# Attention block, one core: normalised rows taken off ScalarE, and the whole plan of instructions replaced

## Chip, core and metric

The kernel runs on one core of one Trainium2 chip. The metric is the device time of one execution in microseconds, from the core's own records. A core has TensorE (PE) for matmuls with a queue of its own for loading weights (PEld), VectorE (DVE), ScalarE (ACT), GpSimd (POOL) and SyncE (SP), which here only issues DMAs. Each engine takes its instructions in order and waits on semaphores where the program says so. Matmul results land in PSUM, which has 8 banks of 512 float32 per partition; everything else lies in SBUF, 128 partitions wide.

## What is computed

One pre-norm transformer layer over 2048 rows of 640 values, with a linear attention of 32 heads of width 20 and a gated bilinear feed-forward of width 1536. Cut to what matters:

```python
def _layernorm(x, axis=-1, eps=1e-5):
    m = jnp.mean(x, axis=axis, keepdims=True)
    v = jnp.var(x, axis=axis, keepdims=True)
    return (x - m) / jnp.sqrt(v + eps)

def _A_ref(x, wqkv, w_phi, wo):          # S = 2048, D = 640, H = 32, Dh = 20
    qkv = (x @ wqkv).reshape(B, S, 3, H, Dh).transpose(2, 0, 3, 1, 4)
    q, k, v = qkv[0], qkv[1], qkv[2]
    pq = jnp.einsum("bhsd,hdf->bhsf", q, w_phi)
    pk = jnp.einsum("bhsd,hdf->bhsf", k, w_phi)
    phi_q = jnp.concatenate([softmax(pq), softmax(-pq)], axis=-1)
    phi_k = jnp.concatenate([softmax(pk), softmax(-pk)], axis=-1)
    kv = jnp.einsum("bhsf,bhsd->bhfd", phi_k, v)
    z  = jnp.einsum("bhsf->bhf", phi_k)
    num = jnp.einsum("bhqf,bhfd->bhqd", phi_q, kv)
    den = jnp.einsum("bhqf,bhf->bhq", phi_q, z)[..., None] + 1e-6
    return (num / den).transpose(0, 2, 1, 3).reshape(B, S, D) @ wo

def _B_ref(x, w_gate, w_up, w_down):      # F = 1536
    return ((x @ w_gate) * (x @ w_up)) @ w_down

h  = x + _A_ref(_layernorm(x), A_wqkv, A_w_phi, A_wo)
h2 = h + _B_ref(_layernorm(h), B_w_gate, B_w_up, B_w_down)
```

All inputs and the output are bfloat16.

## The kernel before

**Tiles and steps.** The 2048 rows are 16 tiles of 128. The program first builds a graph of about a thousand named steps, most of them one instruction, and each with an engine, the buffers that it reads and writes, and sometimes a second engine that can do it as well (`alts`). The table `PLAN` then gives each step by name its place in one common order, which of its engines it runs on (the second field: empty or 0 for the first, 1 for the alternative) and which slots of its pools it uses (the third field: PSUM banks, or slots of ring buffers). `arrange` sorts the steps by place and hands each engine its own list; `emit` works out the semaphore waits from the buffers. So the plan alone sets the order on each engine and on the SP queue, and with the order it sets who waits for whom: an instruction that waits holds up all that stands behind it on its engine.

**Names.** The number behind a name is the row tile. For layer norm: `L1s` (VectorE, two statistics instructions, lines 406 and 407), `L1a` (VectorE, aggregate to mean and variance, line 409), `L1l` and `L1e` (ScalarE, logarithm and exponential that give 1/sqrt, lines 414 and 417, for one, two or four tiles at a time), `L1n` (the shift: minus mean times that factor, one value per row, line 421, GpSimd or VectorE) and `xn` (the normalised row tile, lines 424 to 434). `xn` on VectorE subtracts the mean and multiplies by the factor (line 431), and needs no shift; on ScalarE it is an activation with scale and bias (line 429), and the bias is the shift. Tiles 2 and 9 run on ScalarE in this plan. All tiles from 2 on have a shift, whether or not they use it, and `xn` waits for it as one of its inputs.

`xt` transposes the normalised tile: tiles 0 and 1 on TensorE (line 440, with the evacuation `xte`), the others by a DMA from the SP queue (line 449). That queue also issues the loads of x (`x8` and so on), of the feed-forward weights (`wg`, `wu`, `wd`, line 263) and of `wo`, the transposed loads of the query weights `wqt`, and later the transposes `qT`, `oT` and `hT`.

**The key and value stage.** `WT` and `F1_` fold the feature map w_phi into the key weights (transposes at line 370, folds at line 389, evacuations `WTe` and `Fe1_` at line 229; `Ph` builds the block form of w_phi and `w5` loads it); `F0_` does it for the query weights. `V` and `K` of a tile are ten matmuls each (line 460), for tiles 0 and 1 in five pieces. `Ve` evacuates V (line 229, ScalarE or VectorE). For K come two exponentials on ScalarE (`Kx_0` and `Kx_1`, line 472), a sum on VectorE (`Ks`, line 476), logarithm and exponential on ScalarE (`Kr` and `Ke`, lines 479 and 481, the reciprocal) and a product on GpSimd (`Kn`, line 496). `KV` adds the tile to the 32 heads' state in two PSUM banks that all 16 tiles share (line 504). The buffers of `xn` are four slots, those of the exponentials five.

**The rest.** `Q` has steps of the same kind (`Qx` at lines 529 and 531, `Qs` at 534, `Qr`, `Qb`, `Qe`, `Qn` at 537 to 548, `qT` at 553). Behind `KVe` (line 511), which needs the last `KV`, come `N` (line 566), the division `dd`, `rd`, `o`, the transpose `oT`, `O` (line 603), the sum `h` (line 609), the centred copy `hc` and its transpose `hT`. The feed-forward has five bands of rows; `U` are the gate and up products (line 646), `g` and `u` their evacuations, `D` the down product (line 665), `y` the last sum and `w` the store.

**Where the plan puts the steps that matter below.** TensorE goes through `... V3 K5 V5 K2 V2 V4 F0_0 ...`, later `... K6 K9 Q0 Q1 KV4 K8 KV5 Q5 K11 ...`, and at the end of the stage `KV11 KV12 KV13 KV14 KV15 Q6 N0`. The SP queue goes `... xt6 xt7 x10 x14 wg2 wg0 xt9 wd1 xt8 wg1 xt11 wd0 xt13 xt10 ...`. GpSimd goes `... Kn1 L1n7 L1n6 rqz Kn3 L1n8 L1n9 Kn0 mk0 mk1 Kn2 ...` and ends the stage with `... Kn12 Qb4 Kn14`.

## Time and profile before

| | us |
|---|---|
| three timed runs | 271.76, 271.76, 272.92 |
| median of the three | 271.76 |
| the profiled execution | 272.37 |
| its span, first to last instruction | 270.6 |
| granted TensorE clock over the span | 1.000 |

Times are in microseconds unless marked ns. In a row of the timeline stand the start, the length, the engine, the line of the kernel, the operation, what it writes and reads, the shape, and how many instructions were merged; in brackets how long the engine had been idle before it, and on whom it had waited. Matmuls are pipelined, so their row is longer than the time between two of them. A row of the groups has busy time and mean ns of one instruction, then the idle time just before the group's instructions and who ended most of it. `SPq` is the time in which the SP queue issues a DMA, not the transfer itself. A row of the stretches gives the stretch, its length, and the busy time of PE, PEld, DVE, ACT and POOL with their instructions, then the granted clock, the DMA share and GB/s.

### The profile page before, as it was taken

What the parts mean: (1) busy time and instruction counts of PE and PEld (TensorE: products, weight loads), DVE (VectorE), ACT (ScalarE), POOL (GpSimd) and SP (SyncE); (2) the same over time, 40 slices, a digit from 0 to 9 for tenths busy, and PEclk for the clock granted to TensorE, in tenths of its full rate; (3) what the DMA queues carried; (4) which work ended last, traced back from release to release, by engine and by line L of the source; (5) the groups of instructions that cost most, each with busy time, mean ns of one, the idle gap of its engine ahead of it and who ended that gap; (6) DMA issues with size and microseconds to landing.
All of it is one profiled execution on the core that took longest, in us unless ns stands there. A gap on an engine that the chain in (4) does not pass through costs nothing.

```text
span 270.6 us, 5179 instructions
## 1 busy us (share of the span) xinstructions
PE 263.6 (97%) x2090; PEld 177.4 (66%) x2103; DVE 157.3 (58%) x291; ACT 123.9 (46%) x316; POOL 71.8 (27%) x92
## 2 busy tenths in 40 slices
PE   6999989999999999999999999999999999999996
PEld 4777857777777788765556667765554476544774
DVE  4999799967678998678564252432342411433432
ACT  3899979988876383663531051223122300023000
POOL 6155689999942422205000000000000000000000
DMA  7999996999947997882940000240200001100011
GB/s 210 307 122 172 250 226 132 298 207 253 174 87 145 166 139 133 134 145 55 188 84 2 0 0 25 61 112 1 73 12 2 0 0 51 48 1 0 27 48 61
DMA packets 71752, 28.09 MB, mean 104 GB/s; under 512 B 59056, under 2 KB 71728, under 8 KB 71728
## 3 DMA queue, kind: packets, MB, share of 16 engines
q1 hardware_dynamic: 71440, 27.43, 49.7%
q8 instruction: 16, 0.26, 0.4%
q10 hardware_dynamic: 288, 0.33, 0.3%
q14 instruction: 8, 0.07, 0.1%
HBM read 11.00 MB, written 2.62 MB: 50 GB/s over the span
## 4 chain that ended last, share of the span: by engine, by line
PE 91%; DMA 4%; DVE 2%; ACT 1%; issue 0%; DVEq 0%
PE ps L646 38%; PE ps L460 23%; PE ps L665 19%; PE ps L603 7%; DMA xnT<-xn 3%; PE ps L566 2%; PE ps L504 2%; DMA x_all<-in_A_x_dram 1%; DVE x_all L609 1%; DVE S L534 1%; PE ps L389 1%; DVE st L406 0%; ACT Wp L229 0%; DVE st L407 0%; ACT scratch L229 0%
## 5 line engine op out<-in xcount | busy, mean ns | idle before, releaser
L646 PE MATMUL ps<-xnT,Wgu 128*128 128x512 bf16 (+1 forms) x587 | 106.0, 335 | 0.7
L646 PEld LDWEIGHTS ps<-xnT,Wgu 128*128 128x128 bf16 x600 | 58.2, 98 | 43.5
L651 ACT ACTIVATE gt<-ps 128x512 bf16<-128x512 f32 (+1 forms) x60 | 29.7, 509 | 100.9 <-PE ps L646 62.9
L460 PE MATMUL ps<-Wp,xnT 128*128 128x320 bf16 (+1 forms) x480 | 68.9, 299 | 1.1 <-DMA xnT<-xn 1.1
L460 PEld LDWEIGHTS ps<-Wp,xnT 128*128 128x128 bf16 x480 | 45.3, 97 | 18.7 <-DMA xnT<-xn 1.7
L654 DVE TENSOR_TENSOR ev<-ps,gt 128x512 bf16<-128x512 f32 (+1 forms) x60 | 33.6, 580 | 36.5 <-PE ps L646 27.8
L665 PE MATMUL ps<-Wd,ev 128*128 128x320 bf16 (+2 forms) x396 | 53.9, 295 | 0.0
L665 PEld LDWEIGHTS ps<-Wd,ev 128*128 128x128 bf16 x396 | 38.1, 98 | 15.3 <-DVE ev L654 0.2
L677 DVE SCALAR_TENSOR_TENSOR Wp<-ps,rs,x_all 128x640 bf16<-128x640 f32 (+3 forms) x18 | 14.6, 810 | 49.3 <-PE ps L665 49.1
L496 POOL TENSOR_TENSOR ek<-ek,SR 128x1280 bf16<-128x1280 bf16 x16 | 37.6, 2356 | 5.5 <-ACT SR L481 5.5
L534 DVE TENSOR_REDUCE S<-ph 128x66 f32<-128x1320 bf16 x16 | 23.9, 1517 | 4.6 <-ACT ph L531 4.5
L476 DVE TENSOR_REDUCE SR<-ek 128x64 f32<-128x1280 bf16 x16 | 23.3, 1470 | 3.0 <-ACT ek L472 3.0
L529 ACT ACTIVATE ph<-ps 128x600 bf16<-128x600 f32 x32 | 21.4, 682 | 7.8 <-PE ps L460 7.1
L603 PE MATMUL ps<-Wo,Wp 128*128 128x320 bf16 x160 | 23.7, 299 | 0.1
L548 POOL TENSOR_TENSOR ph<-ph,RQ 128x660 bf16<-128x660 bf16 x16 | 20.7, 1307 | 8.7 <-ACT RQ L544 8.4
L472 ACT ACTIVATE ek<-ps 128x640 bf16<-128x640 f32 x32 | 21.3, 720 | 3.3 <-PE ps L460 2.6
L624 POOL TENSOR_SCALAR ln<-mv 128x1 f32<-128x1 f32 x12 | 2.3, 190 | 75.7 <-ACT ek L620 75.1
L603 PEld LDWEIGHTS ps<-Wo,Wp 128*128 128x128 bf16 x160 | 15.4, 98 | 6.1 <-issue 0.2
L609 DVE SCALAR_TENSOR_TENSOR x_all<-ps,x_all 128x640 bf16<-128x640 f32 x16 | 13.1, 821 | 6.1 <-PE ps L603 6.1
L593 DVE TENSOR_TENSOR o<-ps,sm 128x660 bf16<-128x660 f32 x16 | 13.4, 840 | 1.0 <-ACT sm L586 0.6
L620 ACT ACTIVATE ek<-x_all,mv 128x640 bf16<-128x640 bf16 x16 | 13.1, 820 | 0.0
L229 ACT ACTIVATE ev<-ps 128x640 bf16<-128x640 f32 x16 | 11.2, 705 | 1.3 <-PE ps L460 1.3
(68 smaller groups left out, 158.1 us busy)
## 6 DMA issues: line engine op xcount, KB each, us to landing
out_dram<-Wp SPq DMA_DIRECT2D x15, 160.0 KB, 1.8
x_all<-in_A_x_dram SPq DMA_DIRECT2D x6, 320.0 KB, 4.5
Wgu<-in_B_w_gate_dram SPq DMA_DIRECT2D x4, 480.0 KB, 6.7
Wd<-in_B_w_down_dram SPq DMA_DIRECT2D x4, 480.0 KB, 5.0
Wgu<-in_B_w_up_dram SPq DMA_DIRECT2D x4, 480.0 KB, 5.7
Wp<-in_A_wqkv_dram SPq DMA_DIRECT2D x5, 160.0 KB, 4.7
ev<-in_A_wqkv_dram SPq DMA_DIRECT2D x4, 160.0 KB, 3.7
x_all<-in_A_x_dram SPq DMA_DIRECT2D x3, 160.0 KB, 3.3
```

Of the source, the lines that this page charges most:

```text
L460: ins = e.matmul(pb(b, hb)[:, 0:n1 - n0], lhsT=T["xnT"][:, NC - 1 - c, P * t:P * (t + 1)], rhs=T["Wp"][:, POS[kind], c, n0:n1], start=(c = ...
L472: G.op("act", "%sx%d_%d" % (nm, t, s), lambda e, s=s, b=b, ek=ek: e.activation(out=T["ek"][:, ek.slots[0], 0:2 * D].rearrange("p (b h s f) ...
L476: G.op("dve", "%ss%d" % (nm, t), lambda e, ek=ek, sr=sr: e.tensor_reduce(out=T["SR"][:, sr.slots[0], 0, :], in_=T["ek"][:, ek.slots[0], 0: ...
L496: G.op("pool", "Kn%d" % t, lambda e, eng, ek=ek, sr=sr: e.tensor_tensor(out=T["ek"][:, ek.slots[0], 0:2 * D].rearrange("p (h f) -> p h f", ...
L529: e.activation(out=v[:, 0:10].rearrange("p (b g) j f -> p b g j f", b=2), in_=pp(b, 0, 300).rearrange("p b (g j f) -> p b g j f", j=3, f=D ...
L534: G.op("dve", "Qs%d" % t, lambda e, t=t, ph=ph: e.tensor_reduce(out=T["S"][:, t, 0:66].rearrange("p (g k) -> p g k", k=6), in_=pv(ph).rear ...
L548: return e.tensor_tensor(out=v, in0=v, in1=T["RQ"][:, rq.slots[0], 1, 0:33].rearrange("p (g j) -> p g j", j=3).unsqueeze(3).to_broadcast([ ...
L603: ins = e.matmul(pb(b, hb)[:, 0:320], lhsT=T["oT"][:, oT.slots[0], c, :], rhs=T["Wo"][:, c, 320 * hb:320 * (hb + 1)], start=(c == 0), stop ...
L646: ins = e.matmul(pb(b)[:, 0:n], lhsT=T["Wgu"][:, gu, c, P * ft:P * (ft + 1)], rhs=T["xnT"][:, NC - 1 - c, o0:o0 + n], start=(c == 0), stop ...
L651: G.op("act", "g%d_%d" % (bi, ft), lambda e, pg=pg, gt=gt, n=n: e.activation(out=T["gt"][:, gt.slots[0], 0:n], in_=pb(pg)[:, 0:n], func=AF ...
L654: o_ = G.op("dve", "u%d_%d" % (bi, ft), lambda e, pu=pu, gt=gt, hh=hh, ft=ft, n=n: e.tensor_tensor(out=T["hh"][:, hh.slots[0], ft, 0:n], i ...
L665: ins = e.matmul(pb(b, hb)[:, 0:w], lhsT=T["hh"][:, hh.slots[0], ft, P * tt:P * (tt + 1)], rhs=T["Wd"][:, ft, c0 + w * hb:c0 + w * (hb + 1 ...
```

## The change

Three things. `xn` loses its ScalarE form; its alternative engine is now GpSimd, with the same instruction as on VectorE. The shift steps `L1n` (14 of them), their buffer and `xn`'s wait for them are gone. And `PLAN` is replaced as a whole: 1014 steps instead of 1028.

In the new plan `xn4` and `xn6` run on GpSimd and all other rows on VectorE. ScalarE's queue issues the loads `x1 x3 wk1 w5` (it had `x1 wk3`). `Ve8`, `Ve10`, `Ve11`, `Ve14` and `Ve15` move from ScalarE to VectorE; `WTe0` moves to ScalarE, `xte1` and `Ph1` to VectorE; some of `Fe0_`, `hc` and the small `L2v` change places too. TensorE has the same 295 steps in another order. It starts with `V0_0 V0_1 F1_2 V0_2 K1_0 ...` behind the first four folds, then `K3 V3 K5 V5 V2 K2 V4 F0_0 F0_2 V6 ...`, `... K6 KV2 F0_1 K9 KV3 Q1 Q0 ... K8 KV5 Q5 K11 V9 Q3 Q9 ...`. ScalarE goes `... Ve3 L1l6 Kr0 L1e6 Kx5_0 Kr1 Kx5_1 L1l8 Ke0 Ve5 L1e8 Ve2 Ke1 Ve1 Kx2_0 ...`, VectorE `... WTe4 xte1 xte0 WTe2 xn3 L1s4 L1s5 L1a4 L1a5 xn5 L1s2 L1a2 L1s7 L1s6 xn2 L1a7 L1s9 L1a6 Ks0 L1s8 Ks1 xn7 L1a8 L1a9 Ks3 ...`, GpSimd `... phz ekz xn4 xn6 mk0 Kn0 Kn1 Kn3 mk1 Kn2 mk2 Kn4 Kn5 Kn7 Kn6 Qb1 Kn9 ...` up to `Kn13 Kn12 Kn14`, and the SP queue `... xt6 xt7 x14 x10 wo0 xt9 wu1 xt8 wu2 wd1 wg0 xt11 wg3 xt10 ...`. From `KV11` to `N0` TensorE's order is the old one, and so are its last seven steps.

The plan's lines with the first steps and with the steps named in the prediction, and then the code:

```diff
--- before.py
+++ after.py
-x0:0 x1:1:1 ekz:2 zero:3 id0:4 warm0:5 wk3:6:1 x3:7:1 warm1:8 id1:9 warm2:10 w5:11:1 warm3:12 va1:13 warm4:14 warm5:15 wk0:16:1 warm6:17 warm7:18 eps:19
...
-Ks1:123::0 K0_3:124 L1e2:125 Ve0:126::0 V1_2:127 L1n2:128 xt5:129 V1_3:130 Sz:131 L1n4:132 xn2:133:1:0 V1_4:134 K3:135::4 L1s6:136 Kr1:137 wqt0:138 Ke1:139
...
-L1e6:156 wqt2:157 Ve3:158::2 L1n7:159 L1n6:160 rqz:161 Kx0_0:162::2 V5:163::0 xn7:164::2 Kx0_1:165 xt4:166 xn6:167::3 Kx5_0:168::3 L1a8:169 K2:170::6 L1a9:171
-Ks0:172::2 Kx5_1:173 wqt3:174 Kr3:175 Ke3:176 V2:177::2 Ve5:178::3 Kn3:179 Ks5:180::3 xt6:181 Kx2_0:182::4 Kx2_1:183 V4:184::4 L1s12:185 xt7:186 Ve2:187::4
-L1l8:188 Ks2:189::0 L1e8:190 Kr0:191 F0_0:192::0 L1n8:193 x10:194 Ke0:195 F0_2:196::6 L1n9:197 Ve4:198::5 Kn0:199 V6:200::2 x14:201 L1s13:202 Fe0_0:203
-wg2:204 xn9:205:1:0 wg0:206 F0_4:207::4 K4:208::0 Kr5:209 Fe0_4:210:1 xt9:211 Ve6:212::6 mk0:213 Kr2:214 mk1:215 Ke2:216 Fe0_2:217 KV0:218::4,5 Kn2:219
...
-L1s15:251 Kr4:252 Ve7:253::7 K9:254::6 L1n10:255:1 L1a13:256 Ke4:257 xn11:258::3 Kx6_0:259::4 L1a15:260 L1a12:261 xt11:262 Kx6_1:263 Ks7:264::2 Kn4:265
...
+zero:0 va1:1 x0:2 x1:3:1 warm0:4 x3:5 wk4:6:1 warm1:7 warm2:8 eps:9 gl0:10 wk3:11 wk1:12:1 warm3:13 id0:14 warm4:15 warm5:16 w5:17 wk0:18:1 gla:19 warm6:20
...
+L1a7:139 L1s9:140 xt2:141 L1a6:142 V3:143::0 Ks0:144::0 Kx3_0:145::4 Kx3_1:146 xt4:147 K5:148::6 L1s8:149 Ve3:150::1 L1l6:151 wqt0:152 Ks1:153::1 Kr0:154
...
+mk0:171 Kn0:172 K2:173::6 L1e8:174 Ve2:175::3 L1s13:176 xt6:177 Ke1:178 Ve1:179::4 Ks5:180::3 V4:181::4 Kx2_0:182::3 xt7:183 Kx2_1:184 Kn1:185 L1s12:186
...
+K4:203::6 Ke2:204 xn9:205::3 Ve6:206::6 Fe0_3:207:1 xt9:208 Ke5:209 Fe0_0:210:1 KV0:211::0,1 KV1:212 mk1:213 Kx4_0:214::1 wu1:215 K7:216::4 Kn2:217 xt8:218
...
+wg0:235 L1s11:236 Ke4:237 KV2:238 Kn4:239 F0_1:240::6 Kx6_0:241::3 K9:242::2 L1s14:243 Kx6_1:244 L1a12:245 L1a11:246 Fe0_1:247 L1a10:248 Ks7:249::0 KV3:250
...
+Ks6:266::1 L1l12:267 Q1_4:268 xt11:269 Ke7:270 Q0_2:271 Qx1_0:272::4 KV4:273 Q0_3:274 Kn7:275 Qx1_1:276 Q0_4:277 Ks9:278::2 K8:279::2 Kr6:280 Qx0_0:281::1
...
@@ -244,7 +244,6 @@
     st_b = [Buf("st%d" % t) for t in range(NT)]
     mv_b = [Buf("mv%d" % t) for t in range(NT)]
     rs_b = [Buf("rs%d" % t) for t in range(NT)]
-    nb_b = [Buf("nb%d" % t) for t in range(NT)]
     wkn_b = [Buf("wkn%d" % i) for i in range(NC)]
     wkt_b = [Buf("wkt%d" % i) for i in range(NC)]
     wqt_b = [Buf("wqt%d" % g) for g in range(NC)]
@@ -416,22 +415,14 @@
              [lb], 10 * a - 26)
         G.op("act", "L1e%d" % a, lambda e, a=a, z=z: e.activation(out=T["rs"][:, a:z], in_=T["ln"][:, a:z], func=AF.Exp,
                                                                  scale=-0.5), 0.1, LA, [lb], [rs_b[t] for t in tl], 10 * a - 26)
-        for t in tl:
-            if t > 1:
-                G.op("pool", "L1n%d" % t, lambda e, eng, t=t: e.tensor_scalar(
-                    out=T["nb"][:, t:t + 1], in0=T["mv"][:, t, 0:1], scalar1=T["rs"][:, t:t + 1], scalar2=-1.0, op0=ALU.mult,
-                    op1=ALU.mult), 0.2, LP, [rs_b[t], mv_b[t]], [nb_b[t]], 10 * t - 25, alts=[("dve", 0.07, LD)])
     KVB = [Buf("kvps%d" % k, "psum") for k in range(2)]
     for t in range(NT):
         xb = Buf("xn%d" % t, "xn")
         def xn(e, eng="dve", t=t, xb=xb):
-            if eng == "act":
-                return e.activation(out=rev(xb), in_=T["x"][:, t, :].rearrange("p (c n) -> p c n", c=NC), func=AF.Identity,
-                                    scale=T["rs"][:, t:t + 1], bias=T["nb"][:, t:t + 1])
             return e.tensor_scalar(out=rev(xb), in0=T["x"][:, t, :].rearrange("p (c n) -> p c n", c=NC),
                                    scalar1=T["mv"][:, t, 0:1], scalar2=T["rs"][:, t:t + 1], op0=ALU.subtract, op1=ALU.mult)
-        G.op("dve", "xn%d" % t, xn, 0.5, LD, [x_b[t], mv_b[t], rs_b[t], nb_b[t]], [xb], 10 * t - 22,
-             alts=[] if t < 2 else [("act", act_c(640, True), LA)])
+        G.op("dve", "xn%d" % t, xn, 0.5, LD, [x_b[t], mv_b[t], rs_b[t]], [xb], 10 * t - 22,
+             alts=[] if t < 2 else [("pool", 0.95, LP)])
         if t in TPE:
             b = Buf("pxt%d" % t, "psum")
             def xt(e, t=t, b=b, xb=xb):
@@ -827,7 +818,6 @@
         T["mv"] = sb([P, NT, 2], FP32, "mv")
         T["mv2"] = sb([P, NT, 2], FP32, "mv2")
         T["ln"] = sb([P, NT], FP32, "ln")
-        T["nb"] = sb([P, NT], FP32, "nb")
         T["rs"] = sb([P, NT], FP32, "rs")
         T["rs2"] = sb([P, NT], FP32, "rs2")
         T["SR"] = sb([P, NSLOTS["SR"], 2, 2 * H], FP32, "SR")
```

More of the change, by code (lines that the diff above doesn't have):

```diff
@@ L122 @@
[L122 to L123 removed]
+zero:0 va1:1 x0:2 x1:3:1 warm0:4 x3:5 wk4:6:1 warm1:7 warm2:8 eps:9 gl0:10 wk3:11 wk1:12:1 warm3:13 id0:14 warm4:15 warm5:16 w5:17 wk0:18:1 gla:19 warm6:20
+id1:21 warm7:22 wk2:23:1 warm8:24::4 glb:25 warm9:26 rqz:27 smz:28 wv1:29 Sz:30 warm10:31 warm11:32 wv0:33:1 warm12:34 L1s0:35 warm13:36 x4:37 warm14:38
@@ new lines @@
+mk0:171 Kn0:172 K2:173::6 L1e8:174 Ve2:175::3 L1s13:176 xt6:177 Ke1:178 Ve1:179::4 Ks5:180::3 V4:181::4 Kx2_0:182::3 xt7:183 Kx2_1:184 Kn1:185 L1s12:186
+F0_0:187::2 Kr5:188 Kr3:189 Ve4:190::5 F0_2:191::6 x14:192 Ks2:193::0 V6:194::0 Ke3:195 x10:196 Fe0_2:197 wo0:198 Kn3:199 xn8:200::1 F0_3:201::4 Kr2:202
+K4:203::6 Ke2:204 xn9:205::3 Ve6:206::6 Fe0_3:207:1 xt9:208 Ke5:209 Fe0_0:210:1 KV0:211::0,1 KV1:212 mk1:213 Kx4_0:214::1 wu1:215 K7:216::4 Kn2:217 xt8:218
+Kx4_1:219 Ks4:220::1 V7:221::6 Kx7_0:222::0 wu2:223 Kx7_1:224 wd1:225 mk2:226 L1s10:227 F0_4:228::2 Ve7:229::4 K6:230::4 L1s15:231 Fe0_4:232 Kr4:233 L1a15:234
@@ new lines @@
+Qx10_0:421::0 Qx10_1:422 V14:423::2 Kr14:424 Kn12:425 Qx13_0:426::1 Qs10:427 Qe4:428 V12:429::6 Ve14:430:1:3 Qr10:431::1 qT5:432::4 Ke14:433 Qx13_1:434
+Kn14:435 V15:436::2 Ve12:437::2 Qs13:438 wg1:439 KV11:440 Ve15:441:1:4 KV12:442 Qr13:443::0 KV13:444 Qb13:445 Qb10:446 Qe13:447 KV14:448 Qn4:449 KV15:450
+Q6:451::2 KVe0:452 Qn13:453 KVe1:454 Qx6_0:455::2 N0:456::4 N2:457::0 qT4:458::2 dd0:459::0 Qx6_1:460 Q7:461::6 rd0:462 dd2:463::1 o0:464::0 rl2:465 rd2:466
+o2:467::1 N1:468::2 Qx7_0:469::5 Q11:470::4 dd1:471::1 oT0:472::0 Qx7_1:473 rd1:474 o1:475::2 Q8:476::0 Qx11_0:477::3 oT2:478::1 Qs7:479 Qx11_1:480 N3:481::2
```

120 lines of the change are left out of this document (57 added, 63 removed).

## The prediction

> **What bounds the kernel now.** I read the page first, then the timeline of TensorE, then the timelines of the engines and of the DMA queue that feed it in the first 80 us.
>
> ```profile
> span 270.6 us, 5179 instructions
> PE 263.6 (97%) x2090; PEld 177.4 (66%) x2103; DVE 157.3 (58%) x291; ACT 123.9 (46%) x316; POOL 71.8 (27%) x92
> PE 91%; DMA 4%; DVE 2%; ACT 1%; issue 0%; DVEq 0%
> ...
> 7.12 0.45 PE L440 MATMUL ps<-ident,xn 128*128 128x128 bf16 x5 [0.72 <-DVE xn L431]
> ...
> 10.27 0.48 PE L389 MATMUL ps<-Phi,scratch 128*128 128x140 bf16 x6 [0.19 <-ACT Wp L229]
> 10.58 15.23 PE L460 MATMUL ps<-Wp,xnT 128*128 128x320 bf16 x110
> ...
> 24.28 1.20 PEld L460 LDWEIGHTS ps<-Wp,xnT 128*128 128x128 bf16 x10 [0.28 <-DMA xnT<-xn]
> ...
> 36.63 4.26 PE L460 MATMUL ps<-Wp,xnT 128*128 128x320 bf16 x30 [1.07 <-DMA xnT<-xn]
> 36.62 3.38 PEld L460 LDWEIGHTS ps<-Wp,xnT 128*128 128x128 bf16 x26 [1.40 <-DMA xnT<-xn]
> ...
> 250.04 18.20 PE L665 MATMUL ps<-Wd,ev 128*128 128x320 bf16 x144
> ```
>
> TensorE is 97% busy and is 91% of the chain that ended last. From 10.58 us to 268.24 (250.04 + 18.20) it streams with only two waits worth a name: 0.28 us at 24.28 (step V4 waits for the transposed rows of tile 4) and 1.40 us on the weight loads at 36.62 (step K9 waits for those of tile 9; about 1.36 net, as two steps stand about 0.04 apart anyway). The new order has the same 295 TensorE steps and the same matmuls. So the change can win only what those waits and the first 10.6 us hold, about 2 us, and can lose by any new wait.
>
> **The change, part by part, in its arithmetic.**
>
> ```profile
> L431 DVE TENSOR_SCALAR xn<-x_all,mv,rs 128x640 bf16<-128x640 bf16 x14 | 8.1, 587 | 0.3
> L421 POOL TENSOR_SCALAR nb<-mv,rs 128x1 f32<-128x1 f32 x9 | 2.3, 265 | 10.5 <-ACT rs L417 10.5
> L429 ACT ACTIVATE xn<-x_all,nb,rs 128x640 bf16<-128x640 bf16 x2 | 1.8, 912 | 0.0
> L421 DVE TENSOR_SCALAR nb<-mv,rs 128x1 f32<-128x1 f32 x5 | 1.0, 203 | 0.0
> L548 POOL TENSOR_TENSOR ph<-ph,RQ 128x660 bf16<-128x660 bf16 x16 | 20.7, 1307 | 8.7 <-ACT RQ L544 8.4
> L229 ACT ACTIVATE ev<-ps 128x640 bf16<-128x640 f32 x16 | 11.2, 705 | 1.3 <-PE ps L460 1.3
> L476 DVE TENSOR_REDUCE SR<-ek 128x64 f32<-128x1280 bf16 x16 | 23.3, 1470 | 3.0 <-ACT ek L472 3.0
> ```
>
> Removed: 14 shifts (9 on GpSimd, 2.3 us; 5 on VectorE, 1.0 us) and 2 rows on ScalarE (1.8 us). VectorE keeps 14 rows of 0.59 us: it takes over tiles 2 and 9 from ScalarE and gives 4 and 6 to GpSimd. A GpSimd row isn't in the trace. It costs more than the 0.27 us of a one-element GpSimd instruction and not more than the 1.31 us of a two-input one of 660 elements; I take 1.0, as it has one big input. By itself none of this is on TensorE's path: the rows of tiles 4 and 6 are needed at 24 and 26 us. The plan also moves five evacuations of V (tiles 8, 10, 11, 14, 15) from ScalarE (0.70 us each) to VectorE. They are covered: VectorE stands idle 2.43, 1.83 and 2.12 us between 58 and 71 us (rows below), against 5 x 0.82 = 4.1. Without that cover VectorE would be late by up to 4.1 us for the key sums. What decides is the new order.
>
> ```profile
> 60.08 1.53 DVE L534 TENSOR_REDUCE S<-ph 128x66 f32<-128x1320 bf16 x1 [2.43 <-ACT ph L531]
> ...
> 64.97 1.49 DVE L476 TENSOR_REDUCE SR<-ek 128x64 f32<-128x1280 bf16 x1 [1.83 <-ACT ek L472]
> ...
> 71.39 2.96 DVE L534 TENSOR_REDUCE S<-ph 128x66 f32<-128x1320 bf16 x2 [2.12 <-ACT ph L531]
> ...
> 28.17 0.82 DVE L229 CAST Wp<-ps 128x640 bf16<-128x640 f32 x1 [0.65 <-PE ps L389]
> ```
>
> *Start (to 10.6 us).* ScalarE's queue now issues four loads instead of two, so key weights are queued earlier; but the first rows still wait for the first x (2.90 us of VectorE's idle time, all before 3.96), and then for two statistics and ScalarE's two small steps. The last fold now stands behind two V pieces (2 x 0.27 us) that are work anyway. One evacuation more in line on VectorE, one fewer wait on ScalarE: I take +0.1. Bounds: -0.7 (all of the 0.72 wait at 7.12 gone) and +0.7 (one more ScalarE evacuation of 0.70 in line).
>
> *K2 and V4 (22 to 25 us).* ScalarE now has the logarithm of tile 1's sums (Kr1) ahead of the second exponential of K5, and the statistics of tiles 8 and 9 (L1l8) ahead of the evacuations of V5 and V2. Both wait for VectorE, and everything behind them in ScalarE's queue waits too: K2 and V4 take over those PSUM banks.
>
> ```profile
> 9.90 0.48 DVE L406 BATCH_NORM_STATS2 st<-x_all 128x6 f32<-128x320 bf16 x1
> 10.30 0.48 DVE L407 BATCH_NORM_STATS2 st<-x_all 128x6 f32<-128x320 bf16 x1
> ...
> 22.44 0.29 ACT L479 ACTIVATE SR<-SR 128x64 f32<-128x64 f32 x1
> 22.76 0.26 ACT L481 ACTIVATE SR<-SR 128x64 f32<-128x64 f32 x1
> 22.92 0.69 ACT L229 ACTIVATE ev<-ps 128x640 bf16<-128x640 f32 x1
> 23.50 1.29 ACT L472 ACTIVATE ek<-ps 128x640 bf16<-128x640 f32 x2
> ```
>
> VectorE begins the statistics of tile 4 at 9.90 now; a part of Phi more stands ahead of them (Ph1) and the start is +0.1 late, so I take 10.5. Up to the end of Ks1 stand seven pairs of statistics (0.79 each, from 9.90 to 10.69), five aggregates (about 0.17), two rows and two sums: 5.5 + 0.85 + 1.2 + 2.9 = 10.5, and about 0.9 of waits for ScalarE: Ks1 ends near 21.9. Then Kr1 0.25 and the exponential 0.6 to 0.7: K2's banks are free at 22.9, where TensorE comes at 22.7. Ks1 plus a row and two aggregates gives 22.8 for L1l8; by the starts above (0.3, 0.16, 0.58, 0.2, 0.6 to 0.7) the evacuation of V2 ends at 24.95. V4 starts there instead of at 24.28: +0.7. Bounds 0 and +1.5 (one sum more on VectorE's queue).
>
> *K9 (36.6 us).* The rows of tile 9 are transposed on the SP queue.
>
> ```profile
> 25.66 1.27 SPq L263 DMA_DIRECT2D x_all<-in_A_x_dram  x2
> 26.98 2.14 SPq L263 DMA_DIRECT2D Wgu<-in_B_w_gate_dram  x2
> 29.17 3.40 SPq L449 DMA_TRANSPOSE xnT<-xn  x1
> ...
> xnT<-xn SPq DMA_TRANSPOSE x30, 3.3
> ...
> GB/s 210 307 122 172 250 226 132 298 207 253 174 87 145 166 139 133 134 145 55 188 84 2 0 0 25 61 112 1 73 12 2 0 0 51 48 1 0 27 48 61
> ```
>
> Now 960 KB of gate weights stand ahead of that transpose, in the new order 320 KB of Wo. 640 KB less, at the 250 to 307 GB/s of the busiest slices, is 2.1 to 2.6 us; the row itself, now on VectorE behind Ks2 and tile 8, is ready near 30, and 30 plus the usual 3.3 to landing is 33.5. TensorE comes at 35.25 + 0.8 = 36.05, so the wait is gone: -1.36. Bounds -1.36 and 0. Tile 11's transpose then stands behind three weight loads, where it had one; in the bytes queued ahead in all it is 320 KB worse, 1.0 to 1.3 us, against some 1 us by which TensorE was late for it: 0, at worst +0.9.
>
> *GpSimd (23 to 74 us).*
>
> ```profile
> 16.86 2.36 POOL L496 TENSOR_TENSOR ek<-ek,SR 128x1280 bf16<-128x1280 bf16 x1 [1.17 <-ACT SR L481]
> 23.10 2.35 POOL L496 TENSOR_TENSOR ek<-ek,SR 128x1280 bf16<-128x1280 bf16 x1 [2.85 <-ACT SR L481]
> 26.36 2.36 POOL L496 TENSOR_TENSOR ek<-ek,SR 128x1280 bf16<-128x1280 bf16 x1
> 34.34 4.67 POOL L496 TENSOR_TENSOR ek<-ek,SR 128x1280 bf16<-128x1280 bf16 x2
> 40.53 4.67 POOL L496 TENSOR_TENSOR ek<-ek,SR 128x1280 bf16<-128x1280 bf16 x2 [0.74 <-ACT SR L481]
> 71.70 2.36 POOL L496 TENSOR_TENSOR ek<-ek,SR 128x1280 bf16<-128x1280 bf16 x1
> ```
>
> This engine sets a second limit. Its last normalisation before KV14 (Kn14) ends at 74.06, and KV14, near the end of the 55 matmuls that start at 73.05, comes right behind. Two normalisations run before 26.36 today; in the new order none does, since Kn0 is first and waits for its reciprocal behind L1l8, till about 23.6. Eight of them are done today at 45.20; new: 23.6 + 8 x 2.33 + 0.6 (masks) + 2.2 (waits for K4 and K6) = 45.0. From there to Kn14 both orders have the same work, so Kn14 ends 73.2 to 73.9. TensorE comes at 74.1 - 0.55 = 73.55: +0.1. Bounds -0.9 and +1.9: they are the rivals.
>
> *Behind 76 us.* Same work, N, O, U and D steps reordered; I followed the attention tail up to the first U steps and found waits of 0.1 to 0.3 us at N7 and at two U steps against about as much now. From 140 us on VectorE and ScalarE are at half load or less. I take 0; bounds -0.4 and +0.8.
>
> ```profile
> 140.00:150.00 10.00, 9.95 (x66) 6.38 (x66) 4.77 (x9) 0.98 (x2) 0.00 (x0) 1.00 0.10 20
> ```
>
> Sum: +0.1 + 0.7 - 1.36 + 0 + 0.1 + 0 = -0.46. The profiled execution took 272.37 us (span 270.6 and 1.8 around it), which would make 271.9. The three timed runs have a median of 271.76; against that, **271.3 us**.
>
> **A rule against the change.**
>
> ```profile
> 35.59 0.55 DVE L431 TENSOR_SCALAR xn<-x_all,mv,rs 128x640 bf16<-128x640 bf16 x1
> ```
>
> This VectorE row ran its usual 0.55 us in the middle of GpSimd's 4.67 us from 34.34 on. The Trainium skill, SBUF — State Buffer, section "SBUF: two separate sides", says that VectorE (in a two-port mode or with two SBUF inputs) and GpSimd hold a shared pair of ports as an exclusive lock for a whole instruction, and the loser waits. By that rule the row above would have ended past 36.6; the trace doesn't agree. Were it to hold for the new GpSimd rows, the last rival below would come about.
>
> **Rivals.**
> 1. Faster: no wait at K2 and V4 (Ks1 half a us earlier than I have it), and GpSimd without its 2.2 us of waits: Kn14 then ends by 72.6, TensorE is 1.5 us ahead at KV14 and keeps it: 270.3. For it: VectorE's idle times. Against it: GpSimd's waits come from the K steps' order, which is nearly the old one.
> 2. Slower: GpSimd becomes the bound of the key stage. Its place is KV14; it decides from the point where Kn0 starts after 24.3. If VectorE and ScalarE release Kn0 only at 26.4, where it starts today, 26.4 + 16 x 2.33 + 6 x 1.31 + 7 x 0.24 + 0.6 + 2.2 of waits is 76.0, and all of TensorE's later work shifts by 1.9: 273.7. For it: both normalisations that are early today now come late. Against it: only the 0.7 us of margin that I worked out.
> 3. The wait of K9 only moves on to K11 (tile 11 behind three loads): +0.9, 272.2.
> 4. Each GpSimd row stops VectorE for up to 1.31 us before Ks1: +2.6 there, of which K9's wait hides 0.6: +2.0, 273.3.
>
> **Numbers.** Forecast 0.38, rival 1 0.20, rival 2 0.27, rival 3 0.11, rival 4 0.04. About 0.5% (1.4 us) can be told from no change here, so faster means under 270.4, slower over 273.1. Rival 1 gives most of "faster" and the forecast's lower edge a little: 0.22. Rivals 2 and 4 and the forecast's upper edge give slower: 0.33. The rest, 0.45, is the same. The forecast's own range is 270.3 to 272.6; with the rivals, 269.9 to 274.5.
>
> **What would show it.** Right: no idle time of over 0.3 us before K9; a wait of TensorE of about 0.7 between 22 and 26 us, released by ScalarE; Kn0 starting at 23 to 24.3; Kn14 ending within 0.5 us of 73.6; GpSimd's rows near 1.0 us, and no VectorE row longer under them. Wrong: TensorE's first projection off by more than 0.7 from 10.6; a wait of over 0.5 at K11 or K15; Kn14 past 75; or new waits behind 76 us, where I followed the order least closely.

## The result, and the profile after

| | before | after |
|---|---|---|
| median of 18 runs each, us | 271.56 | 273.16 |
| lowest to highest, us | 270.68 to 273.46 | 272.04 to 273.97 |
| the profiled execution, us | 272.37 | 272.83 |
| its span, us | 270.6 | 271.1 |

The ratio after to before is 1.0049, with a 95% interval of 1.0034 to 1.0064: the change costs 0.9 to 1.7 us, 1.3 in the middle. Ratios leave out disturbed runs, medians here do not. The two profiled executions differ by 0.5 us only, since the one of before lies 0.8 above its median and the one of after 0.3 below: what a run of after usually loses has to be looked for in more profiles than these two.

The page after: the span, TensorE's busy time, and the chain that ended last by engine.

```profile
span 271.1 us, 5163 instructions
PE 264.4 (98%) x2089; PEld 177.8 (66%) x2103; DVE 159.5 (59%) x297; ACT 117.9 (43%) x308; POOL 73.0 (27%) x80
PE 83%; DVE 6%; ACT 5%; DMA 4%; issue 1%; POOL 1%; ACTq 0%; DVEq 0%
```

TensorE was 91% of that chain and is 83%: the work of other engines has come into it, nearly all of it ahead of 45 us. TensorE's timeline after: the rows with a wait, the last fold, and the row at which the last 55 `KV` matmuls of the stage begin:

```profile
9.30 1.45 PE L388 MATMUL ps<-Phi,scratch 128*128 128x140 bf16 x24 [1.03 <-POOL Phi L357]
...
11.22 0.48 PE L388 MATMUL ps<-Phi,scratch 128*128 128x140 bf16 x6
...
26.70 0.80 PE L388 MATMUL ps<-Phi,scratch 128*128 128x140 bf16 x12 [0.61 <-ACT SR L470]
...
44.84 5.62 PE L451 MATMUL ps<-Wp,xnT 128*128 128x320 bf16 x40 [0.73 <-DMA xnT<-xn]
...
73.76 1.86 PE L495 MATMUL ps<-ev,ek 128*128 128x63 bf16 x55
```

The last fold starts at 11.22 (10.27 before, now with 0.5 us of V0 ahead of it). The waits at V4 and K9 are gone. In their place stand one before the first fold F1_3 (1.03 us), one before F0_0 (0.61; 0.91 on the weight loads) and one before K11 (0.73; 1.06 on the weight loads). Both plans have the same TensorE work ahead of KV11, so the last row can be compared: it started at 73.05 before and starts at 73.76 now. The pieces of the chain that release the first and the last of these waits (start, length, what):

```profile
2.22 5.54 DMA w<-in_A_w_phi_dram
...
7.84 1.41 POOL Phi L357 x2
...
39.54 5.25 DMA xnT<-xn
```

The load `w5` of w_phi, which ScalarE's queue issues at 2.22, lands 5.54 us later, at 7.76; GpSimd's two products for Phi end at 9.25, and only then can the first fold start.

### The profile page after: what moved, and what is told of

It reads as the page before. It is cut to its first block, busy times and chain, and to the rows that moved or that the text cites. A ratio compares the mean times of both kernels' runs of the same rounds, so it can differ in the third digit from the quotient of the medians.

```text
span 271.1 us, 5163 instructions
## 1 busy us (share of the span) xinstructions
PE 264.4 (98%) x2089; PEld 177.8 (66%) x2103; DVE 159.5 (59%) x297; ACT 117.9 (43%) x308; POOL 73.0 (27%) x80
## 4 chain that ended last, share of the span: by engine, by line
PE 83%; DVE 6%; ACT 5%; DMA 4%; issue 1%; POOL 1%; ACTq 0%; DVEq 0%
PE ps L637 38%; PE ps L656 19%; PE ps L451 15%; PE ps L594 8%; DVE SR L467 2%; DMA w<-in_A_w_phi_dram 2%; DMA xnT<-xn 2%; PE ps L557 2%; PE ps L495 1%; DVE st L406 1%; ACT Wp L229 1%; DVE st L405 1%; ACT ek L463 1%; DVE xn L422 1%; ACT ev L229 1%
## 5 line engine op out<-in xcount | busy, mean ns | idle before, releaser
L615 POOL TENSOR_SCALAR ln<-mv 128x1 f32<-128x1 f32 x8 | 1.5, 190 | 40.5 <-ACT ek L611 40.0
L532 POOL TENSOR_TENSOR RQ<-RQ 128x32 f32<-128x32 f32 x16 | 3.7, 239 | 26.8 <-ACT RQ L528 26.5
```

## Experiments

Each ratio below is against the kernel before, run in turn on the same chip, with its 95% interval.

### Is the profile of before typical, and does the code matter?

`b_again` is the kernel before, unchanged. `b_code` is its order with the code of the change alone:

```diff
-xn2:133:1:0
+xn2:133::0
-xn9:205:1:0
+xn9:205::0
-L1n2 L1n3 L1n4 L1n5 L1n6 L1n7 L1n8 L1n9 L1n10 L1n11 L1n12 L1n13 L1n14 L1n15
```

> The kernel before, unchanged, for a second profile beside the first. The first one was of an execution of 272.37 us, 0.8 us above the median of 18 runs (271.56). Theory: a usual execution has a shorter wait at K9, which hangs on when the transpose of tile 9 lands behind two weight loads; then this profile shows a wait of 0.4 to 1.0 us there in place of 1.36. Rival: the wait at K9 is the same 1.2 to 1.4 us in every execution, and the spread lies elsewhere.

> The kernel before with the code of the change alone: no shift operations, the rows that ScalarE made (xn2 and xn9 of its order) on VectorE, no row on GpSimd, the order of everything else as before. Theory (the start is the cost): within 0.4 us of before, 271.2 to 272.0; one shift of about 0.1 us less on ScalarE for each row and a row of 0.6 more on VectorE both lie beside other work. Rival (VectorE's load in the first 30 us is the cost): 272.3 or more, with V4 or K2 late by 0.7.

`b_again`: 271.76 us, ratio 0.9997 (0.9977 to 1.0018). Weight loads where K9 stands, the one wait of the weight loads that is listed from 30 to 40 us, and the row of TensorE at which KV11 begins:

```profile
33.95 4.10 PEld L460 LDWEIGHTS ps<-Wp,xnT 128*128 128x128 bf16 x31
```

```profile
PEld ps L504 <- POOL ek L496: 0.4, 1, 0.4
```

```profile
72.08 1.98 PE L504 MATMUL ps<-ev,ek 128*128 128x63 bf16 x55
```

The first row runs from 33.95 to 38.05 without a gap that the view shows: in this execution K9 waits for 0.1 us at most, less than the 0.4 to 1.0 expected, since the transpose of tile 9 landed at 35.21 and not at 36.58. `b_code` and, further down, `b_w5act` have the old order there and no wait at K9 either. The wait of 1.40 us, on which the prediction's largest gain rests, was found in one execution of these four. Without it KV11 starts at 72.08, so that against this execution the profile of after is 1.7 us late at KV11, and not 0.7.

`b_code`: 272.02 us, ratio 1.0026 (1.0004 to 1.0048). The code alone, in the old order, brings nothing, and costs 0.1 to 1.3 us if anything; `a_oldstart` below has the same code and shows no such cost. (Its expectation speaks of a shift on ScalarE: the shifts ran on GpSimd and VectorE.)

### Three local repairs

Each puts one suspected load back ahead: `a_w5` brings `w5` to SP's queue, `a_wqt` the query weights `wqt1` ahead of `xt5`, `a_xt11` the transpose `xt11` ahead of two feed-forward weights.

```diff
 a_w5:   SP     -x0 wk4 wk3 wk0 ...          +x0 wk4 w5 wk3 wk0 ...
         ScalarE -x1 x3 wk1 w5               +x1 x3 wk1
 a_wqt:  SP     -xt3 wqt4 xt5 wqt1 ...       +xt3 wqt4 wqt1 xt5 ...
 a_xt11: SP     -xt8 wu2 wd1 wg0 xt11 ...    +xt8 wu2 xt11 wd1 wg0 ...
```

> The changed kernel with the load of w_phi (w5) third on the SP queue, where the kernel before had it, in place of fourth on ScalarE's queue. Theory (the loss is three waits made by the new order of DMAs: w5, wqt1, xt11): w5 lands near 5.3 us in place of 7.76, the 1.2 us wait before the first fold F1_3 goes, the first projection starts 0.3 to 0.5 us earlier, and the median is 0.2 to 0.5 us lower than the changed kernel's 273.16. Rival (GpSimd bounds the key stage): the start is earlier but KV14 is not, median within 0.2 us of 273.16. Rival (w5 is late because of its 40-byte pieces, not of its queue): it lands past 7 us again.

> The changed kernel with the transposed load wqt1 ahead of xt5 on the SP queue, as in the kernel before, so that it is issued while the queue waits for the rows of tile 5. Theory (three waits of the DMA order): wqt3 lands about 1.2 us earlier than 26.35, the 0.88 us wait before F0_0 goes, median 0.5 to 0.9 us lower than 273.16. Rival (GpSimd bounds the key stage): the wait before F0_0 goes and comes back by KV14, median within 0.2 us of 273.16.

> The changed kernel with the transpose of tile 11 ahead of two of the three weight loads that stand before it on the SP queue (wd1 and wg0 now follow it). Theory (three waits of the DMA order): the transpose lands 1 to 3 us earlier than 44.79, the 1.02 us wait before K11 goes, median 0.6 to 1.0 us lower than 273.16. Rival (GpSimd bounds the key stage): Kn14 ends at 74.2 to 74.6 as it does now (74.50) and KV14 waits for it, so that no more than 0.3 us is won.

Ratios 1.005 (1.0018 to 1.0083), 1.0033 (1.0018 to 1.0048) and 1.0049 (1.0028 to 1.0069): none brings the loss back. `a_w5` (median 273.48 us) and `a_xt11` (273.64) miss what was expected; `a_wqt` (272.72) comes within 0.1 us of it, but its interval overlaps that of the changed kernel. In the profiles the wait before K11 is gone in `a_xt11`, and the one before F0_0 is still 0.83 us in `a_wqt`. `a_w5` does not clear `w5`, since it puts it ahead of `wk3`, which TensorE needs second. But `a_wqt` and `a_xt11` have the very start of the changed kernel (their edits come at 13 and 36 us), and so they show it twice more. Loads of the first 9 us, after and then in these two (KB each, median us from issue to landing):

```profile
ev<-in_A_wqkv_dram SPq DMA_DIRECT2D x4, 160.0 KB, 3.9
ev<-in_A_wqkv_dram ACTq DMA_DIRECT2D x1, 160.0 KB, 4.1
w<-in_A_w_phi_dram ACTq DMA_DIRECT2D x1, 25.0 KB, 5.5
```

```profile
ev<-in_A_wqkv_dram SPq DMA_DIRECT2D x4, 160.0 KB, 4.9
ev<-in_A_wqkv_dram ACTq DMA_DIRECT2D x1, 160.0 KB, 5.2
w<-in_A_w_phi_dram ACTq DMA_DIRECT2D x1, 25.0 KB, 6.5
```

```profile
ev<-in_A_wqkv_dram SPq DMA_DIRECT2D x4, 160.0 KB, 4.7
ev<-in_A_wqkv_dram ACTq DMA_DIRECT2D x1, 160.0 KB, 5.2
w<-in_A_w_phi_dram ACTq DMA_DIRECT2D x1, 25.0 KB, 7.5
```

The same view of the profile of before:

```profile
ev<-in_A_wqkv_dram SPq DMA_DIRECT2D x4, 160.0 KB, 3.7
ev<-in_A_wqkv_dram ACTq DMA_DIRECT2D x1, 160.0 KB, 3.7
w<-in_A_w_phi_dram SPq DMA_DIRECT2D x1, 25.0 KB, 3.5
```

The key weights take 3.7 us before (3.8 to 3.9 in `b_again`), and 3.9 to 5.2 with the new start, so that in the profile of after they are hardly late; `w5` takes 3.5 (in `b_again` too), and then 5.5, 6.5 and 7.5. The profile of after is the mildest of three, and that of `a_xt11`, at 276.07 us, is the slowest of its twelve runs. This made the start the main suspect.

### The start of the one plan in the other

The first loads and TensorE's order at the start were exchanged, apart and together (matmuls on zeros, which only keep TensorE busy, are left out of the lists). `a_start` and `b_start` exchange the loads alone (order and queue); `a_oldstart` and `b_newstart` exchange the whole order of every engine and queue up to F1_2 (`b_newstart` stands on `b_code`).

```diff
 loads of before:   SP x0 x3 w5 wk0 wk4 wk1 wk2 x4 wv1 wv0 ...    ScalarE x1 wk3
 loads of after:    SP x0 wk4 wk3 wk0 wk2 wv1 wv0 x4 ...          ScalarE x1 x3 wk1 w5
 TensorE of before: WT3 WT0 xt1 WT4 WT1 F1_0 F1_3 WT2 xt0 F1_1 F1_4 F1_2 K0_0 ...
 TensorE of after:  WT4 WT3 WT1 xt1 WT0 xt0 WT2 F1_3 F1_1 F1_0 F1_4 V0_0 V0_1 F1_2 ...
```

> The changed kernel with the first loads back in the order and on the queues of before: SyncE issues x0 x3 w5 wk0 wk4 wk1 wk2 x4 and the w_v rows, ScalarE x1 and wk3. Everything else is the changed kernel's. Theory (the start is the cost: with the new split w5, wk3 or wk1 land late): w5 lands at 5.2 to 5.5 us, F1_2 starts at 10.2 to 10.6, and the median falls to 271.6 to 272.3. Rival (the 2.50 us rows on GpSimd and the late Kn14 are the cost): the median stays within 0.3 us of 273.2 and KV14 is still at 74.5 or later. Rival (wqt1 behind xt5 is the cost): F0_0 still waits 0.8 or more and the median stays above 272.8.

> The kernel before, with only the first loads put in the changed kernel's order and on its queues (ScalarE x1 x3 wk1 w5, SyncE x0 wk4 wk3 wk0 wk2 and the w_v rows); rows of normalised x stay where they were. Theory (the start is the cost): 0.8 to 1.5 us slower than before, so 272.4 to 273.1, with F1_2 at 11 us or later. Rivals (GpSimd, or the order of the w_q rows): within 0.3 us of before, 271.4 to 271.9.

> The changed kernel with the whole start of before: up to F1_2 every engine and both queues take the order of before (loads, warm-up matmuls, transposes, folds), and from there on the order is the changed kernel's. Theory (the cost is made in the first 11 us, and loads and TensorE's order there belong together): back to 271.3 to 272.2, within 0.5 us of before, and TensorE has lost 3.4 to 3.9 us by 20 us as in the traces of before. Rival (what follows costs: the 2.50 us rows on GpSimd, F0_0's wait, K11's wait): 272.6 or more though the first 11 us are those of before.

> The reverse: the order of before with the change's code alone (the kernel that took 272.02 us), with the changed kernel's start up to F1_2 on every engine and both queues. Theory (the cost is the start): 272.8 to 273.6, with w5 landing at 7.5 us or later. Rival (the cost lies behind the start): 271.6 to 272.3.

| | loads of before | loads of after |
|---|---|---|
| TensorE's start of before | before, 1; `a_oldstart` 0.9987 (0.9971 to 1.0003) | `b_start` 1.0113 (1.0074 to 1.0151) |
| TensorE's start of after | `a_start` 1.0067 (1.0043 to 1.0090) | after 1.0049; `b_newstart` 1.0098 (1.0061 to 1.0135) |

`a_start` missed its expectation, as the loads of before do not fit TensorE's new order: WT4 comes first there, and wk4, fifth on SP's queue, lands at 6.54. `b_start` and `b_newstart` cost more than was expected: their medians are 274.85 and 274.38 us. With the whole start of before the loss is gone, and all that the change does behind 11 us is worth between -0.8 and +0.1 us. The rivals that put the cost behind the start (the GpSimd rows, F0_0, K11) fall as its main cause.

`a_start` shows a second thing. Its nine runs took 272.03, 272.26 and 274.24 us at a granted clock of 1.000, 273.06 at 0.999, and 273.68 to 274.26 in five runs at 0.994. A mean of 0.994 is 0.006 x 270 = 1.6 us of work at full speed. None of the 26 runs of before beside it was under 0.999. So a slower TensorE can come with late loads. In the record of the changed kernel itself only two of 18 executions have 0.994, so this does not show most of its loss.

### Is the slower TensorE the cost?

`a_warm` adds 15 matmuls on zeros to the changed kernel, where TensorE waits for the first loads:

```diff
-warm15 WT4 WT3 warm16 WT1 ... WT2 F1_3
+warm15 2 warm WT4 3 warm WT3 3 warm WT1 ... WT2 8 warm F1_3
```

> The changed kernel with 15 more warm-up matmuls on zeros at the places where TensorE waits for the first loads: 2 ahead of WT4, 3 ahead of WT3, 2 ahead of WT1, 8 ahead of F1_3. Theory (a TensorE that waits there for more than about 1 us then runs its transposes and folds at half speed for 3 to 6 us, as in the traces where F1's 24 matmuls took 2.3 to 2.6 us and not 1.45): the slow executions go, the highest time falls below 273.8 and the median to 272.2 to 272.9. Rival (the late loads alone are the cost, the speed behind them is not): 273.0 to 273.7, the 15 matmuls of 0.11 to 0.21 us each added where nothing was waited for.

273.35 us, ratio 1.0063 (1.0035 to 1.0091), highest 275.78: the theory's numbers are missed. TensorE's timeline in the execution of 275.78, the slowest of twelve:

```profile
4.93 0.74 PE L371 MATMUL ps<-ident,ev 128*128 128x128 bf16 x5
5.47 0.85 PE L351 MATMUL ps<-ev 128*128 128x256 bf16 x3
7.13 0.71 PE L371 MATMUL ps<-ident,ev 128*128 128x128 bf16 x5 [0.81 <-DMA ev<-in_A_wqkv_dram]
...
9.23 0.74 PE L433 MATMUL ps<-ident,xn 128*128 128x128 bf16 x5
...
10.80 0.44 PE L371 MATMUL ps<-ident,ev 128*128 128x128 bf16 x5
```

Five transposes take 0.71 to 0.74 us up to 10 us and 0.44 to 0.45 later. The three matmuls ahead of WT3 were not enough to bridge the wait for wk3 (it landed at 7.08), so TensorE still stood 0.81 us. It was slow ahead of that wait already (the row at 4.93), so the wait did not begin the slow stretch; at most it made it longer. Whether a gapless TensorE would have been fast is therefore not settled by this run, only that this cure does not work: the loads themselves are late.

### Which of the loads?

Two kernels move one load of before to ScalarE's queue, as the changed kernel does; two put loads of the changed kernel back to SP's queue and leave TensorE's order alone.

```diff
 b_w5act:  SP -x0 x3 w5 wk0 wk4 wk1 wk2    +x0 x3 wk0 wk4 wk1 wk2      ScalarE -x1 wk3  +x1 wk3 w5
 b_wk1act: SP -x0 x3 w5 wk0 wk4 wk1 wk2    +x0 x3 w5 wk0 wk4 wk2       ScalarE -x1 wk3  +x1 wk3 wk1
 a_oneq:   SP -x0 wk4 wk3 wk0 wk2          +x0 wk4 wk3 w5 wk1 wk0 wk2  ScalarE -x1 x3 wk1 w5  +x1 x3
 a_wk1:    SP -x0 wk4 wk3 wk0 wk2          +x0 wk4 wk3 wk1 wk0 wk2     ScalarE -x1 x3 wk1 w5  +x1 x3 w5
```

In the expectations (a) stands for the pieces of `w5`, which take turns with large packets, (b) for a move of `wk1` that makes what stands behind it late, and (c) for neither queue mattering.

> The kernel before with one load moved: w5, third on SyncE's queue and issued at 1.72 us, is third on ScalarE's queue and issued there at about the same time. Theory (a) (its 640 pieces of 40 bytes take turns with SyncE's large packets): w5 lands at 6.2 to 8 us and not at 5.2, Phi and the folds behind it are 0.8 to 2 us later, and the time is 272.3 to 273.6. Rival (c): w5 lands by 5.6 and the time is within 0.3 us of before.

> The kernel before with one load moved: wk1, sixth on SyncE's queue, is third on ScalarE's queue. By (b) everything behind it is late: w5, alongside wk1's packets, lands at 6 us or later and the time is 272.0 to 273.2. By (a) the 40-byte pieces are what suffers, here too, since w5 now has wk1 beside it on the other queue: w5 at 5.6 to 6.8, the time 271.9 to 272.8. By (c): w5 stays within 0.3 us of 5.2 and the time within 0.3 us of before.

> The changed kernel with wk1 and w5 back on SyncE's queue: SyncE x0 wk4 wk3 w5 wk1 wk0 wk2, ScalarE x1 x3 alone; TensorE's order stays the changed kernel's. By (a) and (b): w5 lands at 5.4 to 6.0 in each execution, F1_3 no longer waits for Phi, and the time is 271.4 to 272.3. By (c): 272.8 to 273.5, as with the changed kernel's own queues.

> The changed kernel with wk1 alone back on SyncE's queue, fourth there behind wk3; w5 stays on ScalarE's queue, now third. If wk1's place is the cost: WT3 and WT1 wait less than 0.8 each, TensorE keeps its speed, and the time is 271.8 to 272.5 although w5 still lands at 6.5 or later. If w5's place is the cost: 272.8 to 273.5, with F1_3 waiting for Phi by 0.5 or more.

| | ratio to before | interval |
|---|---|---|
| `b_w5act` | 1.0010 | 0.9989 to 1.0031 |
| `b_wk1act` | 1.0037 | 1.0014 to 1.0059 |
| `a_oneq` | 1.0008 | 0.9992 to 1.0024 |
| `a_wk1` | 1.0016 | 0.9990 to 1.0041 |

`a_oneq` settles the main question: with `wk1` and `w5` on SP's queue and TensorE's new order untouched, the loss goes from 1.0049 to 1.0008, 1.1 us. TensorE's new order is not the cost; the place of these two loads on ScalarE's queue is. It is not that they are issued sooner now: on SP's queue they are issued at 2.67 and 2.19, and on ScalarE's, in the changed kernel, at 1.74 and 2.22. The load of `w5` in it (3.7 us, so it lands at 5.90, where it landed at 7.76 to 9.73 in the three profiles above), and the folds, which no longer wait:

```profile
w<-in_A_w_phi_dram SPq DMA_DIRECT2D x1, 25.0 KB, 3.7
```

```profile
8.15 1.59 PE L389 MATMUL ps<-Phi,scratch 128*128 128x140 bf16 x24
```

The reverse: `wk1` alone on ScalarE's queue costs the kernel before 0.4 to 1.6 us. TensorE's timeline there, and the stretches (length, then busy time of PE, PEld, DVE, ACT, POOL, granted clock, DMA share, GB/s):

```profile
7.08 0.58 PE L372 MATMUL ps<-ident,ev 128*128 128x128 bf16 x5 [1.38 <-DMA ev<-in_A_wqkv_dram]
...
9.05 1.41 PE L391 MATMUL ps<-Phi,scratch 128*128 128x140 bf16 x12
```

```profile
5.00:7.00 2.00, 0.67 (x7) 0.39 (x7) 2.00 (x7) 1.08 (x4) 1.12 (x3) 1.00 1.04 349
7.00:9.00 2.00, 1.92 (x20) 1.92 (x21) 1.53 (x5) 1.42 (x6) 1.53 (x4) 0.57 1.06 364
9.00:11.00 2.00, 2.00 (x25) 2.00 (x23) 0.83 (x3) 1.70 (x3) 0.00 (x0) 0.58 0.94 315
```

WT0 waits 1.38 us for wk0, which lands at 7.04 and not at 5.90, now that `wk1` (landed at 6.75) is moved beside it. Behind that wait the granted clock is 0.57 and 0.58 in the two stretches (it is 0.50 from 7.27 to 10.68), and twelve fold matmuls take 1.41 us where they took 0.80. My estimate from the clock is half of 3.41, 1.7 us, more than the wait itself. `w5` lands at 5.81 there, as (a) has it; the time, 273.12 us, is that of (b).

`b_w5act` missed on the time: `w5` does land at 6.80 as expected, but TensorE then waits 0.73 us at one place, its clock holds, and 0.1% is left. So a late load may cost next to nothing, and one that leaves TensorE standing can be paid twice, as in this execution of `b_wk1act`; other waits as long were not (last section). `a_wk1` lies between; that `wk1` is the larger part fits both pairs, but the intervals of `a_wk1` and `a_oneq` overlap, and how the 1.1 us divide between the two loads stays open.

### What the rest of the change is worth, and a kernel that beats both

`a_best` is `a_start` with the moves of `a_wqt` and `a_xt11`; `a_oldbest` is `a_oldstart` with them; `a_oldbest_dve` is that with `xn4` and `xn6` on VectorE; `a_oneq_fix` is `a_oneq` with them, so five loads of the changed kernel moved and nothing else.

```diff
 a_oneq_fix: SP -xt3 wqt4 xt5 wqt1 ...        +xt3 wqt4 wqt1 xt5 ...
             SP -xt8 wu2 wd1 wg0 xt11 ...     +xt8 wu2 xt11 wd1 wg0 ...
 a_oldbest_dve: -xn4:112:1:1 ... xn6:157:1:2  +xn4:133.5::1 ... xn6:158.5::2
```

> The changed kernel with the first loads as before, wqt1 ahead of xt5, and wd1 and wg0 behind xt11 on SyncE's queue. Theory (start, then F0_0's wait for wqt3 and K11's wait for xt11, each worth 0.3 to 1.0 us): 270.4 to 271.5, faster than before and than the first of these kernels by 0.5 or more. Rival (GpSimd's Kn14 bounds the stretch up to 76 us, whatever is won ahead of it): no faster than the kernel with the first loads alone, within 0.2 us of it.

> The changed kernel with the whole start of before, and with wqt1 ahead of xt5 and wd1 and wg0 behind xt11 on SyncE's queue, so that F0_0 and K11 wait less. Theory: 0.3 to 1.0 us below the kernel with the start of before alone, 270.5 to 271.5, so faster than before by 0.2 to 1.0. Rival (GpSimd's chain of Kn rows bounds the stretch to KV14): the same as the kernel with the start of before alone, within 0.2 us.

> The kernel that beat both (start of before, wqt1 ahead of xt5, wd1 and wg0 behind xt11; 0.9978 of before) with the two GpSimd rows on VectorE at the places of their neighbours. If GpSimd's 2.50 us rows cost time (they delay Kn0 and what follows on GpSimd): 0.3 to 0.8 us faster than that kernel, 0.995 to 0.997 of before. If they lie beside other work: within 0.3 us of it, 0.997 to 0.999. If VectorE is the tighter engine there: slower, 0.999 or more, with V4 or K2 late by 0.5.

> The changed kernel with wk1 and w5 back on SyncE's queue, wqt1 ahead of xt5, and wd1 and wg0 behind xt11: five loads moved, no other order touched. If F0_0's and K11's waits for their loads are what is left: 0.3 to 0.7 us below the kernel with wk1 and w5 alone, 0.997 to 0.999 of before. If later waits take that up: 1.000 to 1.002, as with wk1 and w5 alone.

| | median, us | before beside it | ratio | interval |
|---|---|---|---|---|
| `a_best` | 273.33 | 271.59 | 1.0052 | 1.0030 to 1.0074 |
| `a_oldbest` | 271.34 | 272.00 | 0.9978 | 0.9963 to 0.9993 |
| `a_oldbest_dve` | 271.55 | 271.82 | 0.9984 | 0.9970 to 0.9998 |
| `a_oneq_fix` | 271.27 | 271.78 | 0.9987 | 0.9968 to 1.0005 |

`a_best` missed: it has `a_start`'s misfit. `a_oldbest` is faster than before by 0.2 to 1.0 us and than the changed kernel by about 1.9 (0.9978 against 1.0049); it is the one to keep. That the moves of `wqt1` and `xt11` bring something of this is not shown: the intervals with and without them overlap. On VectorE the two rows cost or win nothing that shows. `a_oneq_fix` can't be told from before by its interval. TensorE's timeline in its profiled execution, which took 270.58 us, 0.7 less than its median:

```profile
6.72 0.45 PE L370 MATMUL ps<-ident,ev 128*128 128x128 bf16 x5 [0.76 <-DMA ev<-in_A_wqkv_dram]
...
8.46 1.45 PE L389 MATMUL ps<-Phi,scratch 128*128 128x140 bf16 x24
...
25.30 0.80 PE L389 MATMUL ps<-Phi,scratch 128*128 128x140 bf16 x12
...
71.56 1.86 PE L496 MATMUL ps<-ev,ek 128*128 128x63 bf16 x55
```

No fold waits for Phi, F0_0's wait has fallen to about 0.4 us on the weight loads, K11 does not wait, and KV11 starts at 71.56, 2.2 us ahead of the changed kernel's 73.76.

## Why the prediction was wrong

The time lies inside the range, but the sign is wrong: the forecast was 0.46 us faster than before, and the change is 1.3 us slower. None of the rivals names the cause.

**The step that failed: the start.** The prediction counted ScalarE's queue as a help ("four loads instead of two, so key weights are queued earlier") and took +0.1, with bounds of -0.7 and +0.7. Queued earlier is not landed earlier. The loads put back on one queue bring 1.1 us, the whole start 1.7 (0.9987 against 1.0049), so the term is outside its own bounds. What it left out: a load on the second queue also takes time from those on the first (with `wk1` moved there, `wk0` landed at 7.04 and not at 5.90), and the 640 pieces of `w5` take longer beside large packets (its load took 5.5 to 7.5 us and not 3.5). How much of the loss is the wait for the loads and how much a slower TensorE behind it stays open. The Trainium skill, DMA: Bandwidth & Descriptors, section "Issuing engines are not separate DMA queues", says that DMAs started by the scalar, sync or gpsimd engine all run on the same 16 DMA engines and interleave. The rows of the two queues in the last section agree with it (548 and 674 packets in one stretch). It spoke against counting the second queue as a help, and was not weighed.

**K9, -1.36.** The mechanism was right: the wait is gone. Its size was one execution's. `b_again` has hardly any wait there (0.1 us at most), so against the median there was little to win; the profile that it was read from lay 0.8 us above that median. The prediction did convert its sum to the median, but left the term whole. That the terms behind the start come out nearly right in sum is luck: they were -0.56 together, and `a_oldstart`, with the start of before, is -0.4 (-0.8 to +0.1), though K9 had little to give, K2 and V4 cost nothing and F0_0 did.

**K2 and V4, +0.7.** Wrong place. V4 starts at 24.44 after all, with no wait; Ks1 ended at 21.67 and Kn0 started at 23.17, as worked out (21.9 and 23.6). The steps of ScalarE behind that were added up wrongly: from 22.8 they give 24.7 and not 24.95, and V2's evacuation ended at 24.16. A wait of 0.9 stands right behind V4, at F0_0. The row above names ScalarE, but F0_0 starts about 0.32 us after the query weights `wqt3` land in this profile and by 0.32 to 0.35 in the others with this order of TensorE, early or late as they land. SP's queue after:

```profile
11.60 1.26 SPq L286 DMA_TRANSPOSE scratch<-in_A_wqkv_dram  x1
14.12 1.22 SPq L440 DMA_TRANSPOSE xnT<-xn  x1
15.38 1.27 SPq L286 DMA_TRANSPOSE scratch<-in_A_wqkv_dram  x1
```

The queue stands idle from 12.86 to 14.12, as `xt5` waits for its row and `wqt1` is behind it. Before, `wqt1` was ahead of `xt5`. This is a part of the wait only: with `wqt1` ahead it is 0.28 to 0.51 us in four profiles and 0.83 in `a_wqt`, without it 0.68 to 1.19 in eight. The prediction's rows of SP's queue begin at 25.66 us. So a wait of nearly the size forecast, close to its place and with ScalarE named, is luck.

**K11, 0, and rival 3.** Half right. The profile after has the wait (1.06 on the weight loads, the worst case was +0.9); of the eight profiles with SP's order of the change at that place three have it, at 0.4 to 1.5 us.

**GpSimd, +0.1, and rival 2.** Right on the whole, from a wrong price. GpSimd and VectorE after:

```profile
13.48 0.60 DVE L422 TENSOR_SCALAR xn<-x_all,mv,rs 128x640 bf16<-128x640 bf16 x1 [1.44 <-ACT rs L416]
...
13.56 2.50 POOL L422 TENSOR_SCALAR xn<-x_all,mv,rs 128x640 bf16<-128x640 bf16 x1 [3.37 <-ACT rs L416]
...
20.64 2.50 POOL L422 TENSOR_SCALAR xn<-x_all,mv,rs 128x640 bf16<-128x640 bf16 x1 [4.58 <-ACT rs L416]
...
23.17 6.99 POOL L487 TENSOR_TENSOR ek<-ek,SR 128x1280 bf16<-128x1280 bf16 x3
...
67.52 6.98 POOL L487 TENSOR_TENSOR ek<-ek,SR 128x1280 bf16<-128x1280 bf16 x3
```

A row takes 2.50 us, not the 1.0 taken and outside the bounds of 0.27 to 1.31. It costs little: the second row ends at 23.14 and Kn0 starts at 23.17, while ScalarE's reciprocal for Kn0 was there at 22.88, so the row delays it by 0.3 us, and without both rows on GpSimd nothing is won (0.9984 against 0.9978). Kn14 ends at 74.50 and KV14 runs without a wait; with the start of before Kn14 ended at 73.51, inside the 73.2 to 73.9 worked out. Rival 2, the slower case with the highest chance, falls: `a_oldstart` has the same GpSimd order and no loss.

**Rival 4**, in which a GpSimd row stops VectorE: it falls. VectorE's row at 13.48, and one at 21.59 under the second GpSimd row, took 0.60 us.

**Behind 76 us, 0.** Fair: in the profiles the new order has small waits at N7, a U step and O4 there and no longer those at N5 and O9; `a_oldstart` as a whole is -0.4 us to before.

## What to carry to other kernels

Where a kernel's first work waits for loads, a load that is needed later should stand behind those that are needed first, on their queue; on a second queue it takes turns with them. That is no case against a second queue as such: the kernel before and `a_oneq` both issue two early loads on ScalarE's. A wait of a microsecond or two in the first ten can cost twice, once as the wait and once as a slower TensorE behind it, and need not. And before the removal of a wait is counted as a gain, look at the same wait in a second execution: here the largest term of the sum was a feature of one.
